# Attention units on an even timetable, and the last channel weights rounded at their use

## The chip, the core and the metric

The kernel runs on one core of a Trainium2 chip. A core has five engines with a queue each: PE multiplies matrices (its weight loads are listed apart as PEld), DVE, ACT and POOL work element by element, and SP issues the DMAs here. Each of DVE, ACT, POOL and SP takes its instructions in the order written; an instruction that waits holds up all behind it on its engine. The metric is device time in microseconds of one launch, the median of three runs.

## The reference

Three stages work on a batch of 4 sequences of 768 steps. The first is a gated linear attention with 8 heads of 48 channels, the second a block that mixes along the sequence, the third a mixer of tokens and then of channels.

```python
for t in range(S):                                   # attention, per batch and head
    state = f[t][:, None] * state + outer(k[t], v[t])
    y[t] = q[t] @ state
x = y.transpose(0, 2, 1, 3).reshape(B, S, H * D)     # 384 channels
h = np.maximum(x @ w_in, 0)                          # second stage
u, v = h[..., :512], h[..., 512:]
v_n = (v - mean(v)) / sqrt(var(v) + 1e-6)
v_s = einsum('ts,bsd->btd', w_spatial, v_n) + b_spatial[None, :, None]
x = (u * v_s) @ w_out
xt = x.transpose(0, 2, 1)                            # third stage
u = x + (np.maximum(xt @ w_tok1, 0) @ w_tok2).transpose(0, 2, 1)
out = u + np.maximum(u @ w_ch1, 0) @ w_ch2
```

The weights of the input block, of the output of the second stage, and of the third stage come as 64-bit floats; `f`, `k`, `q`, `v` and `w_spatial` come as 32-bit ones.

## The kernel before

Every product is made of three fp32r matmuls: each operand is split in a rounded part (names ending in `h`) and what is left of it (`l`), and `mm3` (L191, matmuls at L195 to L197) adds h·h, h·l and l·h in PSUM.

**Attention units.** The recurrence is cut into units, one for each batch, half of the sequence (`hf`) and pair of heads (`p`, 0 to 3): 32 units, numbered 0 to 31, eight to a batch. A unit is a Python generator, `att_unit` (L390), with five parts between its yields. Part 1 loads the unit's inputs (`fkq`, L400; with p = 0 also `vt`, L259), takes sigmoids on ACT and two scans on DVE (L269, L274), and scales keys and queries (L277). Part 2 is on PE: transposed keys `pt` (L283) and the products of keys and queries `pa` (L292), which ACT copies and POOL masks (`am`, L296, L297). I call it the unit's keys. Part 3 is PE's products of keys and values `pk` (L306, L307) and on DVE the chain of states `z` and `state` (L316 to L330). Part 4 is PE's product of queries and states, `py` (L338). Part 5 adds masked products times values into the same `py` (L346); I call it the sums. Then ACT and DVE split `py` into two parts (L422, L423). `py` has a single PSUM buffer, so the product with states of one unit waits until DVE has read the sums of the unit before.

**Gap rows.** The units with p = 0, 1, 2 write their 96 rows of `py` straight into the tiles `xh` and `xl` of their half. The rows that 64 - 48 leaves open are filled from the fourth unit: its parts `yh` and `yl` go through 12 DMAs of 16 rows each (L424 to L428), issued by SP. So the first use of a half's `xh` and `xl` waits for these.

**Tiles of the second stage.** For a half of a batch `s1` has three tiles `norm` (L480: nine matmuls of 512 columns into `pv`) and four tiles `gate` (L503: nine of 384 columns into `pu`). For a batch `s23` has eight tiles `mix` (L517: 18 matmuls, `ps`) and six `out1` (L538: 12 matmuls, `px`). That is 28 tiles to a batch. The three PSUM buffers of `ps_m` serve them all; `mix` is read out by DVE, the others by ACT first.

**Order.** PE's order in this part is the order written (`manual_schedule`, L566). `weave` (L183) spreads a list of attention steps over a list of tiles. `joined` (L450) makes two steps for each unit k:

```python
before = [k - 1] * (k > ks[0])
out += [each(*before, k, k + 1), each(k, *before)]
```

The first step runs the product with states of unit k - 1, the keys of unit k and part 1 of unit k + 1; the second runs part 3 of unit k and the sums of unit k - 1. The other engines' order is chosen by the scheduler.

**Weights of 64 bits.** `rounded` (L61) loads a piece of 128 rows (L64), puts its bits together on DVE (L69, L72), scales on ACT (L76) and adds on POOL (L77). Most third-stage weights are rounded early: `round_weight` (L89) makes pieces that store the result in DRAM (L100), and `more` (L461) runs one step of them behind each `gate` and `mix` tile from batch 1 on. Later `split_weight` (L134) loads the 32-bit copy (L153), rounds it to `h` on ACT (L155) and takes the rest `l` on POOL, or on DVE for `wc2` (L159). The staging tiles `wst` and `wsa` have three buffers each.

**Third stage.** `ff` (L699) runs twelve steps for each half: `up1` (`p`, then `hh` on ACT at L711 and `hl` on DVE at L712) and `down` (L724, `po`). POOL looks through all 64-bit weights for values near a threshold in the same steps (`look`, L123, three instructions for each of 88 pieces).

Of the kernel before, what the change touches and what calls it, by code (L numbers as in the profile page):

```python
# [18 lines left out]
def tile_kernel(ctx, tc, fkqs, v, w_in, w_sp, b_sp, w_out, w_t1, w_t2, w_c1, w_c2, out):  # L19
# [23 lines left out]
    def f32(ap):  # L43
        return ap.bitcast(F32)
# [154 lines left out]
    def body(general):  # L199
# [190 lines left out]
        def att_unit(b, hf, p):  # L390

            u = f"{b}{hf}{p}"
            t0 = hf * W
            fkq = at3.tile([P, 3 * W + 1 + NCW], F32, tag="fkq", name=f"fkq{u}")
            if (b, hf, p) == (0, 0, 0):
                for i in (2, 0, 1):
                    x = slice(i * W, (i + 1) * W + (i == 2) * (1 + NCW))
                    nc.sync.dma_start(out=fkq[:, x], in_=fkqs[b, p, hf, :, x])
            else:
                nc.sync.dma_start(out=fkq, in_=fkqs[b, p, hf])  # L400
            if p == 0:
                att_load_v(b, hf)
            fs = at2.tile([P, W + 1], F32, tag="fs", name=f"fs{u}")
            nc.scalar.activation(fs, fkq[:, 2 * W : 3 * W + 1], AF.Sigmoid)
            starts = fs[:, :W:C] if general else first[:, ::C]
            nc.scalar.activation(starts, fkq[:, 3 * W + 1 :], AF.Sigmoid)  # L406
            core = scanned if general else chunked
            py = yield from core(u, b, hf, p, fs, fkq, vts[b, hf])

            if p == 0:  # L410
                xt[b, hf] = (
                    xtp.tile([P, NK, W], F32R, tag="xh", name=f"xh{b}{hf}"),
                    xtp.tile([P, NK, W], F32R, tag="xl", name=f"xl{b}{hf}"),
                )
            xh, xl = xt[b, hf]
            if p < NK:
                yh, yl = xh[:, p, :], xl[:, p, :]
            else:
                yh = attp.tile([P, W], F32R, tag="yh", name=f"yh{u}")
                yl = attp.tile([P, W], F32R, tag="yl", name=f"yl{u}")  # L420
            pyf = py.rearrange("p c t -> p (c t)")
            nc.scalar.copy(yh[:112], pyf[:112])  # L422
            nc.vector.tensor_tensor(out=yl[:112], in0=pyf[:112], in1=f32(yh[:112]), op=ALU.subtract)  # L423
            if p == NK:  # L424
                for src, dst in ((yh, xh), (yl, xl)):
                    for m in range(2 * NK):
                        r0, w0 = 64 * (m // NK) + GAP * (m % NK), D + 64 * (m % 2)
                        nc.sync.dma_start(out=f32(dst[w0 : w0 + GAP, m // 2, :]), in_=f32(src[r0 : r0 + GAP, :]))  # L428

        units = [(b, hf, p) for b in range(B) for hf in range(2) for p in range(NP)]  # L430
        gens = {}
# [15 lines left out]
                out += [each(k + 1), each(k), each(k), each(k, k)]  # L447
            return out

        def joined(ks):  # L450

            out = []
            for k in ks:
                before = [k - 1] * (k > ks[0])
                out += [each(*before, k, k + 1), each(k, *before)]
            return out + [each(ks[-1], ks[-1])]

        st1 = {}
        early = []
# [11 lines left out]
        def s1(b, hf):  # L471
# [6 lines left out]
            d["u", hf] = us = up.tile([P, NJ, W], F32, tag="u", name=f"u{b}{hf}")  # L478

            def norm(i):  # L480
                xh, xl = xt[b, hf]
                ps = ps_m.tile([P, DH], F32, tag="m", name=f"pv{b}{hf}{i}")
                tsl = slice(i * P, (i + 1) * P)
                mm3(ps, [(xh[:, c, tsl], xl[:, c, tsl], winh[:, c, DH:], winl[:, c, DH:]) for c in range(NK)])
# [16 lines left out]
                nc.vector.tensor_tensor(out=d["vl"][:, s, :], in0=vf, in1=f32(d["vh"][:, s, :]), op=ALU.subtract)  # L501

            def gate(j):  # L503
                xh, xl = xt[b, hf]
# [62 lines left out]
        done = 2 * NP  # L567
        second, sa = joined(range(NP, done)), staged(st_a)
        weave(second[:4], sa[:6])
        weave(s1(0, 0), second[4:], sa[6:])  # L570
        out_steps = staged(st_b)
        rest = []
        for name, src in (("wt1", w_t1), ("wt2", w_t2), ("wc1", w_c1), ("wc2", w_c2)):
            kept[name], x = round_weight(wst, src, f"{name}{int(general)}", general)
            early += x
        early[:] = staged(list(early))
        for b in range(B - 1):
            a, (m, last_out) = s1(b, 1), s23(b)
            ks = range(done, done + NP + 1)
            steps = joined(ks)  # L580
            cut = len(steps) * len(a) // len(a + m)
            weave(a, steps[:cut], out_steps if b == 0 else [])
            weave(m, steps[cut:])
            x = s1(b + 1, 0)
            for i, y in enumerate(last_out):
                x.insert(2 + 3 * i, y)
            done = 2 * NP * (b + 2)
            weave(x, joined(range(ks[-1] + 1, done)))
        while early:
            early.pop(0)()  # L590
        right.close()
# [174 lines left out]
        h3p = e(tc.tile_pool(name="h3p", bufs=4))  # L766
        op = e(tc.tile_pool(name="op", bufs=2))
        otp = e(tc.tile_pool(name="otp", bufs=3))
        c2h, c2l, st_c = split_weight(w3p, wst, kept["wc2"], "wc2", NF, DM, nc.vector)
        st_c = staged(by_block[2 * NK : 3 * NK] + st_c[:3] + by_block[3 * NK :] + st_c[3:])  # L770
        weave(c2(0), st_c[:12])
        for b in range(B):
# [65 lines left out]
```

## Time and profile before

| | us |
|---|---|
| median of three runs (840.52 to 844.2) | 844.14 |
| the profiled execution | 838.88 |
| its span, first to last instruction | 837.1 |
| PE busy in the span | 772.7 |
| DVE, ACT, POOL busy | 392.1, 271.6, 365.6 |

The profile page lists the engines' busy time, and the trace can be asked for stretches of the span, for the order in time of one engine, and for what ended each idle time. Busy time of a stretch is no measure of its limit: what counts is which wait ended last. The granted clock of PE is the mean share of full speed in a stretch, between the two levels 1.2 and 2.4 GHz. Up to 47 us the first four units and the input weights are worked on; 47 to 93 us holds the first half of batch 0; then three stretches of eight units and 28 tiles follow, up to 411.9 us; the rest has no attention units.

### The profile page before, as it was taken

How to read it: one execution, taken by the hardware profiler on the slowest of the kernel's cores; microseconds unless marked ns; L12 is line 12 of the kernel's file. 1: busy time of each engine (PE TensorE's matmuls, PEld its weight loads, DVE VectorE, ACT ScalarE, POOL GpSimd, SP SyncE). 2: the span in 40 equal slices, each digit the busy share in tenths (PEclk: the TensorE clock that was granted, in tenths of full speed). 3: DMA queues.
4: the chain of work that ended last, by engine and by line, in shares of the span. 5: the costliest groups of instructions: out<-in, count | busy, mean ns of one | idle time of the engine just before them, and what ended most of it. 6: DMA issues, size and time to landing. Idle time of an engine off the chain costs nothing.

```text
span 837.1 us, 13044 instructions
## 1 busy us (share of the span) xinstructions
PE 772.7 (92%) x4860; PEld 713.9 (85%) x4860; DVE 392.1 (47%) x776; ACT 271.6 (32%) x602; POOL 365.6 (44%) x566
## 2 busy tenths in 40 slices
PE   5879799997979979889799999999999999999996
PEld 3557599885978858778699999999999999999996
DVE  6858467575785757876146251222122212222221
ACT  5556342343434424334353351112111311121110
POOL 3524220131542415424285279365935494547420
PEclk9889899998989979999899999999999999999999
DMA  7653321333646454543253162213221322113111
GB/s 254 192 173 120 100 70 33 125 106 107 190 127 200 137 161 135 178 125 98 81 162 94 58 197 67 85 48 123 85 86 38 115 75 85 48 29 114 38 57 34
DMA packets 53289, 91.06 MB, mean 109 GB/s; under 512 B 6624, under 2 KB 43104, under 8 KB 53216
## 3 DMA queue, kind: packets, MB, share of 16 engines
q1 hardware_dynamic: 53216, 90.14, 34.8%
q8 instruction: 40, 0.66, 0.3%
q14 instruction: 33, 0.27, 0.1%
HBM read 72.02 MB, written 15.73 MB: 105 GB/s over the span
## 4 chain that ended last, share of the span: by engine, by line
PE 71%; DMA 12%; DVE 10%; issue 3%; ACT 1%; POOL 1%; SPq 1%; DVEq 0%; ACTq 0%; POOLq 0%
PE po L724 17%; PE p L197 7%; PE p L195 7%; PE p L196 7%; DMA fkq<-in_fkq 5%; PE ps L195 3%; PE ps L197 2%; PE pa L292 2%; PE ps L196 2%; DMA vt<-in_v 2%; PE py L338 2%; PE pv L197 2%; PE py L346 2%; PE pv L195 2%; PE pv L196 1%
## 5 line engine op out<-in xcount | busy, mean ns | idle before, releaser
L712 DVE SCALAR_TENSOR_TENSOR hl<-p,hh 128x384 fp32r<-128x384 f32 x96 | 53.4, 557 | 187.2 <-ACT hh L711 181.9
L711 ACT ACTIVATE hh<-p 128x384 fp32r<-128x384 f32 x96 | 47.0, 490 | 196.8 <-PE p L197 196.8
L724 PE MATMUL po<-hl,wc2h 128*128 128x384 f32 x288 | 97.3, 338 | 0.4 <-DVE hl L712 0.4
L724 PE MATMUL po<-hh,wc2l 128*128 128x384 f32 x288 | 96.7, 336 | 0.0
L724 PE MATMUL po<-hh,wc2h 128*128 128x384 f32 x288 | 75.1, 337 | 0.1
L195 PE MATMUL ps<-wsph,vh 128*128 128x384 f32 x192 | 68.0, 354 | 0.0
L131 POOL TENSOR_SCALAR look<-look 128x192 f32<-128x192 f32 x88 | 62.8, 714 | 7.6
L197 PE MATMUL ps<-wsph,vl 128*128 128x384 f32 x192 | 65.9, 343 | 0.0
L196 PE MATMUL ps<-wspl,vh 128*128 128x384 f32 x192 | 65.9, 343 | 0.0
L197 PE MATMUL p<-uh,wc1l 128*128 128x384 f32 x192 | 65.0, 338 | 0.0
L130 POOL TENSOR_TENSOR look<-look 128x192 f32<-128x192 f32 x88 | 44.8, 511 | 45.9 <-DMA look<-in_w_c 25.6
L196 PE MATMUL p<-ul,wc1h 128*128 128x384 f32 x192 | 64.7, 337 | 0.0
L195 PE MATMUL p<-uh,wc1h 128*128 128x384 f32 x192 | 64.3, 338 | 0.0
L132 POOL TENSOR_TENSOR lows<-lows,look 128x192 f32<-128x192 f32 x88 | 53.1, 604 | 6.4
L735 POOL TENSOR_TENSOR us<-uh,ul 128x384 f32<-128x384 f32 x24 | 24.1, 1015 | 72.2 <-DVE ul L695 62.7
L297 POOL TENSOR_SCALAR_AFFINE_SELECT am<-am 128x384 f32<-128x384 f32 x64 | 38.7, 620 | 37.9 <-ACT am L296 37.6
L269 DVE TENSOR_TENSOR_SCAN pg<-fs,first 128x384 f32<-128x384 f32 x32 | 31.7, 992 | 50.2 <-ACT first L406 50.2
L724 PEld LDWEIGHTS po<-hl,wc2h 128*128 128x128 f32 x288 | 54.1, 188 | 0.7 <-DVE hl L712 0.7
L724 PEld LDWEIGHTS po<-hh,wc2l 128*128 128x128 f32 x288 | 54.1, 188 | 0.0
L724 PEld LDWEIGHTS po<-hh,wc2h 128*128 128x128 f32 x288 | 52.2, 188 | 0.4 <-ACT hh L711 0.4
L338 PE MATMUL py<-fkq,state 112*112 112x128 f32 x160 | 27.9, 298 | 21.8 <-DVE xl L423 10.8
L338 PEld LDWEIGHTS py<-fkq,state 112*112 112x112 f32 x160 | 23.1, 188 | 28.9 <-DVE xl L423 13.0
(332 smaller groups left out, 1976.9 us busy)
## 6 DMA issues: line engine op xcount, KB each, us to landing
fkq<-in_fkq SPq DMA_DIRECT2D x31, 578.0 KB, 4.1
look<-in_w_c SPq DMA_DIRECT2D x48, 192.0 KB, 2.3
vt<-in_v SPq DMA_DIRECT2D x8, 576.0 KB, 5.9
x1d<-xs SPq DMA_DIRECT2D x24, 192.0 KB, 2.0
xf<-x1d SPq DMA_DIRECT2D x12, 384.0 KB, 4.6
out<-ot SPq DMA_DIRECT2D x24, 192.0 KB, 2.0
look<-in_w_in SPq DMA_DIRECT2D x16, 192.0 KB, 3.2
look<-in_w_t SPq DMA_DIRECT2D x16, 192.0 KB, 2.4
```

The costliest lines, as they stand in the source:

```text
L130: nc.gpsimd.tensor_tensor(out=hi, in0=hi, in1=hi, op=ALU.mult)
L131: nc.gpsimd.tensor_scalar(out=hi, in0=hi, scalar1=NEAR**2, scalar2=None, op0=ALU.is_lt)
L132: nc.gpsimd.tensor_tensor(out=to, in0=to, in1=hi, op=ALU.add)
L195: nc.tensor.matmul(ps, lh, rh, start=first and i == 0, stop=False, **kw)
L196: nc.tensor.matmul(ps, lh, rl, start=False, stop=False, **kw)
L197: nc.tensor.matmul(ps, ll, rh, start=False, stop=i == n - 1, **kw)
L269: nc.vector.tensor_tensor_scan(out=pc, data0=fs[:, :W], data1=first, initial=0.0, op0=ALU.mult, op1=ALU.add)
L297: nc.gpsimd.affine_select(out=am[j], in_=am[j], compare_op=ALU.is_ge, fill=0.0, base=0, pattern=[[0, NCW], [1, C]], channel_multiplier=-1,)
L338: nc.tensor.matmul(py[:112, c, :], now[c][:112, :112], qi[:112, c * C : (c + 1) * C], start=c == n1, stop=False, skip_group_check=True,)
L711: nc.scalar.activation(hh, ps, AF.Relu)
L712: nc.vector.scalar_tensor_tensor(out=hl, in0=ps, scalar=0.0, in1=f32(hh), op0=ALU.max, op1=ALU.subtract)
L724: nc.tensor.matmul(po[c], l[:, ft, csl], r, start=ft == 0 and x == 0, stop=ft == NF - 1 and x == 2)
```

## The change

There are four parts.

1. The attention steps are no longer spread list by list. A timetable `turns` gives each step a tile number; `run` starts what is due before each tile. A batch has 28 tiles (`period`) and eight units, so a unit's first step comes every 3.5 tiles and its second half a unit later. All times are moved forward so that a half's last unit ends some tiles before that half's first `norm`, where before it ended one tile ahead.
2. The product with states (part 4) moves from the first step of a unit (`keys`) into the second (`sums`), right before part 3 of the next unit and its own sums. At the first unit of a batch (`i == 0`) it stays in `keys`, and the sums come there too.
3. `xh` and `xl` become one tile `x` with both parts side by side, and `yh`, `yl` one tile `y`. Six DMAs of 16 rows and both parts take the place of the twelve.
4. `wc2`, 12 pieces, is no longer rounded early and stored. `split_weight` rounds it where it is used, while `c2(0)` and `ff(0, 0)` run.

```diff
-                for src, dst in ((yh, xh), (yl, xl)):
-                    for m in range(2 * NK):
-                        r0, w0 = 64 * (m // NK) + GAP * (m % NK), D + 64 * (m % 2)
-                        nc.sync.dma_start(out=f32(dst[w0 : w0 + GAP, m // 2, :]), in_=f32(src[r0 : r0 + GAP, :]))
+                for m in range(2 * NK):
+                    r0, w0 = 64 * (m // NK) + GAP * (m % NK), D + 64 * (m % 2)
+                    nc.sync.dma_start(out=f32(x[w0 : w0 + GAP, m // 2]), in_=f32(y[r0 : r0 + GAP]))
...
+        def keys(k, before=False):
+
+            return each(*[k - 1] * before, k, *[k - 1] * before, k + 1)
+
+        def sums(k, before=True):
+
+            return each(*[k - 1] * before, k, *[k - 1] * before)
...
+        turns = [(-7, keys(k + 2)), (-6, sums(k + 2)), (-5, keys(k + 3)), (-4, sums(k + 3))]
+        period = 4 * NJ + 4 * NCW
+        for b in range(1, B):
+            for i in range(2 * NP):
+                k = 2 * NP * b + i
+                at = (b - 1) * period + i * period / (2 * NP) - (0 if general else 5)
+                then = at + period / (4 * NP)
+                if k < 2 * NP + 2 and not general:
+                    at, then = 2 * i - 3, 2 * i - 2
+                turns += [(at, keys(k, i == 0)), (then, sums(k, i > 0))]
+        turns += [((B - 1) * period - (0 if general else 5), each(k, k))]
...
+            for m in main:
+                while turns and turns[0][0] <= now[0]:
+                    turns.pop(0)[1]()
+                m()
+                now[0] += 1
...
-        for name, src in (("wt1", w_t1), ("wt2", w_t2), ("wc1", w_c1), ("wc2", w_c2)):
+        for name, src in (("wt1", w_t1), ("wt2", w_t2), ("wc1", w_c1)):
...
-        c2h, c2l, st_c = split_weight(w3p, wst, kept["wc2"], "wc2", NF, DM, nc.vector)
+        c2h, c2l, st_c = split_weight(w3p, wst, w_c2, "wc2", NF, DM, nc.vector, tiny=general)
```

The first place is on PE, in the tiles of batch 0's first half. `state` marks the product with states, `pt` and `pa` the keys, `pk` part 3 and `am` the sums. Before, unit 6's product with states is followed by unit 7's keys, and after a `gate` tile by unit 7's `pk` and unit 6's sums:

```order
L338 MATMUL py_821<-fkq_599,state_129 112x128
L338 MATMUL py_821<-fkq_599,state_130 112x128
L338 MATMUL py_821<-fkq_599,state_127 112x128
L283 MATMUL pt_825<-ident,fkq_703 128x112 x2
L292 MATMUL pa_830<-fkq_703 128x128
...
L195 MATMUL pu_869<-xh_231,winh 128x384
...
L306 MATMUL pk_880<-vt_431,kn_828 64x48
...
L346 MATMUL py_821<-am_691,vt_431 64x128
```

In the changed kernel the same unit's product with states stands behind unit 7's keys and a whole `norm` tile, directly ahead of unit 7's `pk` and its own sums:

```order
L283 MATMUL pt_756<-ident,fkq_659 128x112 x2
L292 MATMUL pa_761<-fkq_659 128x128
...
L195 MATMUL pv_802<-winh,x_231 128x512
...
L338 MATMUL py_826<-fkq_587,state_129 112x128
L338 MATMUL py_826<-fkq_587,state_130 112x128
L338 MATMUL py_826<-fkq_587,state_127 112x128
L306 MATMUL pk_830<-vt_430,kn_759 64x48
...
L346 MATMUL py_826<-am_647,vt_430 64x128
```

Between the sums of one unit and the product with states of the next there is now a full unit's distance; before it was half of one.

The second place is on PE, at the end of batch 0's first half: the sums of unit 7 (`am`), which the gap rows come from, and the first `norm` (`pv`) of the second half. Before, one piece of weights and one `gate` tile stand between them:

```order
L346 MATMUL py_915<-am_833,vt_431 48x128
L163 MATMUL wsppl_942<-wspsa_862,ident 128x384
L164 MATMUL wsppl_942<-wsph,minus 128x384
L195 MATMUL pu_946<-xh_231,winh 128x384
...
L197 MATMUL pu_946<-xh_231,winl 128x384
L195 MATMUL pv_965<-winh,xh_642 128x512
```

In the changed kernel three `gate` tiles (`pu`), four pieces of weights, and work of the units 8 and 9 stand between them:

```order
L346 MATMUL py_868<-am_764,vt_430 48x128
L163 MATMUL wsppl_919<-wspsa_793,ident 128x384
...
L195 MATMUL pu_930<-x_231,winh 128x384
...
L306 MATMUL pk_941<-vt_777,kn_876 64x48
...
L195 MATMUL pu_960<-x_231,winh 128x384
...
L283 MATMUL pt_971<-ident,fkq_907 128x112 x3
...
L195 MATMUL pu_1007<-x_231,winh 128x384
...
L338 MATMUL py_1022<-fkq_775,state_127 112x128
...
L306 MATMUL pk_1025<-vt_777,kn_975 64x48
...
L346 MATMUL py_1022<-am_881,vt_777 48x128
L195 MATMUL pv_1052<-winh,x_634 128x512
```

At the ends of batch 0's second half and of the later halves the distance is of the same kind.

The third place is on DVE, where `ff(0, 0)` begins. Before, the queue holds the `hl` of each step and one instruction (L159) for each piece of `wc2`:

```order
L712 SCALAR_TENSOR_TENSOR hl_5156<-p_5145,hh_5155 128x384
L712 SCALAR_TENSOR_TENSOR hl_5191<-p_5180,hh_5190 128x384
L159 TENSOR_TENSOR wc2l<-wc2sa_5178,wc2h 128x384
...
L159 TENSOR_TENSOR wc2l<-wc2sa_5210,wc2h 128x384
L159 TENSOR_TENSOR wc2l<-wc2sa_5280,wc2h 128x384
L712 SCALAR_TENSOR_TENSOR hl_5225<-p_5214,hh_5224 128x384
```

In the changed kernel the two rounding instructions of each piece (L69, L72) stand among them, and the first of these waits for its piece's DMA:

```order
L732 SCALAR_TENSOR_TENSOR hl_5045<-p_5034,hh_5044 128x384
L715 TENSOR_TENSOR ul_4829<-p_4954,uh_4828 128x384
L69 TENSOR_SCALAR wc2sa_5031<-wc270st 128x384
L72 SCALAR_TENSOR_TENSOR wc2sa_4991<-wc260st,wc2sa_4991 128x384
L159 TENSOR_TENSOR wc2l<-wc2sa_4951,wc2h 128x384
L72 SCALAR_TENSOR_TENSOR wc2sa_5031<-wc270st,wc2sa_5031 128x384
L69 TENSOR_SCALAR wc2sa_5068<-wc280st 128x384
L732 SCALAR_TENSOR_TENSOR hl_5084<-p_5073,hh_5083 128x384
```

Nine of the twelve pieces stand this way among `c2(0)` and `ff(0, 0)`; the first three stand earlier, among the `mix` tiles of batch 3.

## Rows read from the trace of the kernel before

**Rows 1.** The page's part 1: busy us, share, and instructions.

```profile
PE 772.7 (92%) x4860; PEld 713.9 (85%) x4860; DVE 392.1 (47%) x776; ACT 271.6 (32%) x602; POOL 365.6 (44%) x566
```

**Rows 2.** Waits of PE up to 500 us: total us, times, longest.

```profile
PE pv L195 <- DMA xh<-yh: 15.3, 4, 5.5
PE py L338 <- DVE xl L423: 10.8, 7, 3.6
...
PE py L338 <- DVE state L316: 5.9, 4, 3.2
PE py L338 <- DVE yl L423: 4.9, 4, 2.1
PE pv L197 <- DMA xl<-yl: 3.9, 4, 3.0
...
PE wsppl L163 <- DMA wspsa<-in_w_sp: 2.3, 1, 2.3
```

**Rows 3.** Stretches: length, then busy of PE, PEld, DVE, ACT, POOL; PEclk, DMA, GB/s.

```profile
120.19:150.26 30.07, 30.07 (x231) 28.17 (x230) 17.25 (x38) 8.67 (x22) 3.36 (x8) 1.00 0.22 67
93.41:196.18 102.77, 94.91 (x686) 83.25 (x687) 62.44 (x139) 37.88 (x90) 21.19 (x44) 0.96 0.29 89
196.18:306.38 110.20, 98.07 (x674) 85.81 (x675) 77.02 (x159) 43.05 (x98) 41.19 (x67) 0.92 0.50 153
306.38:411.90 105.52, 95.30 (x675) 83.47 (x675) 69.60 (x146) 41.50 (x91) 39.56 (x65) 0.95 0.40 127
```

**Rows 4.** Stretches at the start of the third stage, with the same columns.

```profile
480.00:500.00 20.00, 19.50 (x113) 18.75 (x113) 11.32 (x19) 10.99 (x23) 14.15 (x16) 1.00 0.68 208
500.00:530.00 30.00, 30.00 (x173) 30.00 (x172) 6.77 (x13) 4.42 (x9) 21.78 (x36) 1.00 0.31 86
```

**Rows 5.** PE in order of time, 84 to 110 us: start, us, instruction, idle before.

```profile
85.20 0.87 PE L346 MATMUL py<-am,vt 128*64 128x128 f32 x12
...
93.41 0.76 PE L195 MATMUL pv<-winh,xh 128*128 128x512 f32 x1 [4.76 <-DMA xh<-yh]
...
96.28 0.63 PE L197 MATMUL pv<-winh,xl 128*128 128x512 f32 x1
96.70 0.63 PE L195 MATMUL pv<-winh,xh 128*128 128x512 f32 x1
...
100.25 0.40 PE L195 MATMUL pv<-winh,xh 128*128 128x512 f32 x1
100.48 0.40 PE L196 MATMUL pv<-winl,xh 128*128 128x512 f32 x1
...
107.76 0.34 PE L196 MATMUL pu<-xl,winh 128*128 128x384 f32 x1
107.93 0.34 PE L197 MATMUL pu<-xh,winl 128*128 128x384 f32 x1
```

**Rows 6.** SP's DMA issues at the end of batch 0's first half.

```profile
87.31 3.68 SPq L428 DMA_DIRECT2D xh<-yh  x6
91.15 4.81 SPq L428 DMA_DIRECT2D xl<-yl  x6
```

**Rows 7.** DVE at 55 us, the remainder of a unit's sums.

```profile
55.77 0.56 DVE L423 TENSOR_TENSOR xl<-py,xh 112x384 fp32r<-112x384 f32 x1
```

**Rows 8.** Longest rounding instructions of a weight piece on DVE, 95 to 420 us.

```profile
L72 DVE SCALAR_TENSOR_TENSOR wc10da<-wc10d01152st,wc10da 128x384 uint32<-128x384 uint32 x1 | 1.4, 1384 | 0.0
...
L69 DVE TENSOR_SCALAR wc20da<-wc20d30st 128x384 uint32<-128x384 uint32 x1 | 1.2, 1171 | 0.5 <-POOL am L297 0.5
```

**Rows 9.** The same on POOL, 196 to 306 us.

```profile
L77 POOL TENSOR_TENSOR wt20da<-wt20da,wt20d00st 128x384 uint32<-128x384 uint32 x1 | 1.9, 1887 | 1.1 <-ACT wt20d00st L76 1.1
```

**Rows 10.** Instructions on wc2h: ns shortest, median, longest.

```profile
L155 ACT CAST wc2h<-wc2sa x12: 502/513/517, 474.5 to 496.6; 128x384 fp32r<-128x384 f32 x12
L159 DVE TENSOR_TENSOR wc2l<-wc2sa,wc2h x12: 540/558/1391, 475.1 to 497.1; 128x384 fp32r<-128x384 f32 x12
```

**Rows 11.** The chain that ended last: a load of a 64-bit piece on it.

```profile
348.33 5.09 DMA wc20d60st<-in_w_c
```

More of the change, by code (lines that the diff above doesn't have):

```diff
@@ L410, in att_unit @@
             if p == 0:
[L411 to L420, printed above, removed]
+                xt[b, hf] = xtp.tile([P, NK, 2, W], F32R, tag="x", name=f"x{b}{hf}")
+            x = xt[b, hf]
+            y = x[:, p] if p < NK else attp.tile([P, 2, W], F32R, tag="y", name=f"y{u}")
+            yh, yl = y[:, 0, :], y[:, 1, :]
             pyf = py.rearrange("p c t -> p (c t)")
@@ L448, in apart @@
             return out
[L450 to L456, printed above, removed]
+        def keys(k, before=False):
+            return each(*[k - 1] * before, k, *[k - 1] * before, k + 1)
+        def sums(k, before=True):
+            return each(*[k - 1] * before, k, *[k - 1] * before)
         st1 = {}
@@ L480, in norm @@
             def norm(i):
-                xh, xl = xt[b, hf]
+                xh, xl = (xt[b, hf][:, :, k, :] for k in range(2))
                 ps = ps_m.tile([P, DH], F32, tag="m", name=f"pv{b}{hf}{i}")
@@ L503, in gate @@
             def gate(j):
-                xh, xl = xt[b, hf]
+                xh, xl = (xt[b, hf][:, :, k, :] for k in range(2))
                 ps = ps_m.tile([P, W], F32, tag="m", name=f"pu{b}{hf}{j}")
@@ L566, in body, with run, also @@
         ordered.enter_context(tc.manual_schedule(engines={mybir.EngineType.PE}))
[L567 to L570, printed above, removed]
+        k = NP
+        sa = staged(st_a)
+        weave([keys(k), sums(k, False), keys(k + 1), sums(k + 1)], sa[:6])
+        turns = [(-7, keys(k + 2)), (-6, sums(k + 2)), (-5, keys(k + 3)), (-4, sums(k + 3))]
[9 more added lines that the diff above has]
+        turns += [((B - 1) * period - (0 if general else 5), each(k, k))]
+        now = [-7]
+        def run(main):
+            for m in main:
[3 more added lines that the diff above has]
+                now[0] += 1
+        def also(main, filler):
+            return [
+                lambda n=n, m=m: [
+                    x() for x in filler[len(filler) * n // len(main) : len(filler) * (n + 1) // len(main)] + [m]
+                ]
+                for n, m in enumerate(main)
+            ]
+        run(also(s1(0, 0), sa[6:]))
         out_steps = staged(st_b)
-        rest = []
-        for name, src in (("wt1", w_t1), ("wt2", w_t2), ("wc1", w_c1), ("wc2", w_c2)):
+        for name, src in (("wt1", w_t1), ("wt2", w_t2), ("wc1", w_c1)):
             kept[name], x = round_weight(wst, src, f"{name}{int(general)}", general)
@@ L578, in body @@
             a, (m, last_out) = s1(b, 1), s23(b)
[L579 to L583, printed above, removed]
+            run(also(a, out_steps if b == 0 else []))
+            run(m)
             x = s1(b + 1, 0)
@@ L586, in body @@
                 x.insert(2 + 3 * i, y)
-            done = 2 * NP * (b + 2)
-            weave(x, joined(range(ks[-1] + 1, done)))
+            run(x)
+        while turns:
+            turns.pop(0)[1]()
         while early:
```

## The prediction

> **What bounds the kernel now.** I began with the page's busy times: PE is busy for 772.7 of 837.1 us [rows 1], far ahead of the others, so the kernel is a stream of matmuls, and what can be won is PE's 64 us of idleness and whatever makes its matmuls slow. Next came the waits of PE [rows 2]. Two kinds stand out. The first `norm` of a half waits for the gap rows, on four occasions each for `xh` and `xl`: 15.3 + 3.9 = 19.2 us. The product with states (L338) waits for DVE, for the `xl` or `yl` that frees `py` and for `state`: 10.8 + 4.9 + 5.9 = 21.6 us. All of it lies in the first 500 us; behind that PE is full [rows 4].
>
> The third reading is how fast the matmuls go. Behind the wait of 4.76 us at 93.41, matmuls of 512 columns start 0.42 us apart; from about 100 us on it is 0.23 [rows 5]. That is the lower of the two clock levels, then the upper. The stretches show it as well: 1.00 where PE was never idle, but 0.96, 0.92 and 0.95 over the three stretches of eight units, whose waits fall in between [rows 3]. So a long wait costs twice: its own length, and slow matmuls behind it.
>
> **The change part by part.** *Gap rows.* Before, one `gate` tile (9 x 0.17 = 1.6 us [rows 5]) and at batch 0 one weight piece stand between the fourth unit's sums and `norm`. SP alone needs 3.68 us for six issues and 4.81 for the other six [rows 6]. After, six issues carry both parts, so some 4.8 us at most, plus the split ahead of them and the landing behind. The order gives three `gate` tiles, units' work and weight pieces as distance at batch 0 (4.7 us of `gate` alone, and about 10 with the rest), and two `out1` tiles (12 matmuls of 0.17, 2.1 us each) beside three `gate` tiles and units' work at the others, 9 to 10 us. The sums ended at 85.20 + 0.87 = 86.07 [rows 5], the first issue came 1.2 us later [rows 6], and `norm` began 7.3 us behind the sums with the first six landed. With both parts in six issues some 8 us are needed, the second part being 0.56 later on DVE [rows 7]; that fits with 1 to 2 us to spare. What would be late next is SP's queue: the `fkq` and `vt` loads stand ahead of the six issues, as before. I take all 19.2 us; the bounds are 10 (half of the waits return) and 19.2.
>
> *Product with states.* Its two needs, `py` read out and `state` computed, were met half a unit ahead; now a unit, 11 us at 28 tiles a batch. The longest wait seen was 3.6 us [rows 2], so the added half unit covers it. I take all 21.6, with 10 as the lower bound. Where a batch begins, however, the product follows the previous sums after one tile (1.6 us of `gate`). The read-out alone takes some 0.5 us on ACT and 0.56 on DVE [rows 7], and DVE has `z` and `state` in between. I put 1 us on each of four such places, 4 in all; bounds 0 and 4 x 3.6 = 14.
>
> *The wait for `w_spatial`* (2.3 us [rows 2]) came from twelve gap issues ahead of a load on SP; the load now stands ahead of six. I take 2.3. In exchange unit 5's keys now stand ahead of unit 4's product, at a place where DVE may not be ready: between 0 and the longest wait for DVE, 3.6 [rows 2]; I take 2.
>
> *Slow matmuls.* From the clock column the lost share is 0.04 x 102.8 + 0.08 x 110.2 + 0.05 x 105.5 = 18.2 us [rows 3]; part of that lies in the waits themselves. From the work it is more. The clean stretch of 30.07 us holds five `mix`, three `out1` and three units; at 0.174 a matmul the tiles make 126 x 0.174 = 21.9, which leaves 2.7 a unit; I use 2.9, for units of the second half have a third state. A batch then needs 288 x 0.174 + 54 x 0.23 + 8 x 2.9 = 85.7 us of PE. PE was busy 94.9, 98.1 and 95.3, together 288.3, against 257 and about 4 for four pieces of `w_out`: 27 us more. The bounds are thus 3 (if every idle us was slow) and 27; I take 18, nearer to the second. A clock that stays at 1.00 for 30 us with PE full says that it needs no rest.
>
> *DVE as the next limit.* In batch 1's stretch DVE is busy for 77 of 110.2 us [rows 3], and it has the same work there after. If PE needs 86, DVE stands at 90%, in order, with rounding pieces whose first instruction waits for a load of up to 5.1 us [rows 11]. PE's distances of 11 us take most of this. I put 5 us on it, bounds 0 and 12 (the idleness of that stretch now). In batch 2 the pieces of `wc2` leave DVE.
>
> *`wc2` at its use.* Twelve stores and reads of 32-bit copies go; twelve times L69, L72, L76, L77 come to the start of the third stage. DVE is busy there for 11.3 of 20 us and 6.8 of 30 [rows 4]. Nine pieces bring 9 x 2 x 0.56 = 10 us by the median of an instruction of that size [rows 10], at most 9 x (1.38 + 1.17) = 23 [rows 8]. Three staging buffers hold a piece from load to POOL's add: 5.1 + 1.2 + 1.4 + 1.9 = 9.6 at the longest [rows 8, 9, 11], 3.2 per piece, against a step of `ff` of 18 matmuls, 3.1. So it about keeps up at the worst, and the pieces start six tiles early. PE's small wait for `hl` there, 0.4, may become some us: taken at 2, bounds -0.4 and 8.
>
> Here the Trainium skill speaks against the change. The rows show that an L159 of 0.56 us at the median took up to 1.39 [rows 10], and POOL is busy for 21.8 of 30 us [rows 4]. The page "SBUF — State Buffer", section "Who interferes with whom", says that a DVE instruction with two inputs in SBUF and a POOL instruction that reads SBUF exclude each other, the later one waiting for the whole of the other. L72 has two such inputs, and is moved to where POOL is busiest. By that rule the nine pieces cost DVE 23 us rather than 10; the trace agrees with it in the longest rows, but the median doesn't show it.
>
> *Leftovers.* 2 us for the clock behind new waits.
>
> The sum: 19.2 + 21.6 + 2.3 + 18 = 61.1 us gained; 4 + 2 + 5 + 2 + 2 = 15 given back; net 46.1. The profiled execution took 838.88, so 792.8. That execution lies 5.3 under the median of the runs and 1.6 under the lowest; halfway, 3.4 on top makes 796.2, say 796.
>
> **The rivals.** *DVE's queue takes the waits over.* The distances help only if DVE works off its queue in time; if its in-order loads hold it in batches 0 to 2, half of the 21.6 and a third of the 18 are won, and the new costs come at 10 and not 5: 19.2 + 10.8 + 2.3 + 6 - 20 = 18.3, which gives 820.6 and with the 3.4 on top 824. For it speaks 77 of 110 busy; against it that PE was never idle from 120 to 150, and that the units are now as far apart as they can be. Chance 0.12.
>
> *The `ff` start is crowded.* DVE spends 23 us rather than 10 on the pieces, `hl` comes late for five or six steps, and PE waits 8 us and is slow behind it for 4: 12 in place of 2, so 806. For it: the longest rows and POOL's load; against: the margin, since the last piece is needed eleven steps of 3.1 us behind the first. Chance 0.12.
>
> *Slower.* The pieces of `wc2` go through one after the other: if the three buffers are held by pieces that wait for each other's turn on DVE, POOL and SP, each takes load, rounding, add, copy and remainder, 5.1 + 1.2 + 1.4 + 1.9 + 0.5 + 1.4 = 11.5 us, against a step of 3.1: nine pieces then cost 9 x 8.4 = 75 us. With the 46.1 + 2 won, that is 27 slower than the profiled execution, 870 with the 3.4. It decides from 3.1 + 48 / 9 = 8.4 us a piece. Against it speaks that three buffers exist and the queues interleave. Chance 0.03.
>
> *The change doesn't do what it says.* The order shows the distances, so only a wait that these don't touch can undo it, say SP's queue being late with `fkq`, so that keys wait where sums did: all of 21.6 and 18 would be given back, and 838.9 - 21.5 + 15 = 832.4, 836 with the 3.4. Chance 0.05.
>
> **How the numbers follow.** The forecast has 0.68. All kind bounds at once would gain 70 us and give back nothing, 772; they won't meet, and I set its lower end at 779. Its upper end is 812, with the lower bound of the gap rows or of the product with states, or DVE's 12. The crowded start lies inside these. The range is 779 to 825, which takes in the DVE rival; outside are the slower one, the undone change and the forecast's tails, under 0.2. About 0.5% can be told from no change here, 4.2 us: faster means under 839.9. The forecast, both middle rivals and half of the last are faster, 0.94; within 0.5% is 0.03, the rest of the last; slower is 0.03.
>
> **What the profile will show.** The first `norm` of the four halves starts without a wait for the gap DMA, and six issues take 3.7 to 4.8 us. L338's waits fall from 21.6 to some 4, and what is left sits one tile behind a batch's beginning. PEclk is 0.98 or more in the three stretches, and these take 90 to 95 us each. The last unit's sums end well ahead of 411 us, at some 360. Between there and the end PE is full but for a few us at the start of `ff(0, 0)`. It would be wrong if L338 or the keys wait for DVE in batch 1, if `norm` waits for SP, or if `hl` waits behind L69.

## The result, and the profile after

The changed kernel takes 799.65 us (median of four runs, 797.51 to 802.19) against 843.32 us (median of four; the 844.14 of the table is that of the first three); the ratio is 0.9489, with an interval of 0.9445 to 0.9532. The forecast was 796, in a range of 779 to 825. The profiled execution took 802.19 us, with a span of 800.5, so it is one of the longer runs; on another chip, beside the experiments, the same kernel took 797.73 (797.55 to 798.87).

Part 1 of the page, as in [rows 1]: PE is busy 16 us less for the same 4860 matmuls, since fewer of them run at the lower clock, and idle for 44 us in place of 64.

```profile
PE 756.9 (95%) x4860; PEld 709.4 (89%) x4860; DVE 406.6 (51%) x776; ACT 269.9 (34%) x602; POOL 370.8 (46%) x556
```

The waits of PE behind 40 us (total, times, longest), which answer to [rows 2]; these are the first three of eleven. In the rows, L417 is what L423 was, L744 what L724 was, and L732 what L712 was:

```profile
PE py L338 <- DVE x L417: 9.3, 4, 6.9
PE pt L283 <- issue: 3.0, 1, 3.0
PE po L744 <- DVE hl L732: 2.3, 2, 1.5
```

The waits for gap rows and for `w_spatial` are gone, and none for `state` is left. The eight that are not shown, 7.9 us together and none above 1.9, are waits for DVE or ACT at other instructions; the kernel before has none of them. Of the four waits for DVE's remainder one makes up most: 6.9 us.

The three stretches between the first `norm` tiles of the second halves, as in [rows 3] (length, busy PE, PEld, DVE, ACT, POOL, PEclk, DMA share, GB/s), then two short ones around that wait:

```profile
90.24:183.05 92.81, 90.11 (x659) 81.36 (x659) 64.54 (x136) 38.63 (x92) 27.02 (x45) 1.00 0.31 95
183.05:288.93 105.88, 95.30 (x675) 85.72 (x675) 79.17 (x160) 42.27 (x98) 41.78 (x68) 0.92 0.51 158
288.93:373.75 84.82, 84.82 (x634) 78.25 (x634) 55.21 (x117) 35.34 (x80) 23.95 (x42) 1.00 0.31 92
...
260.00:270.96 10.96, 3.94 (x38) 3.19 (x36) 9.35 (x22) 5.33 (x14) 5.38 (x9) 0.79 0.38 130
271.00:280.00 9.00, 9.00 (x45) 8.17 (x46) 7.93 (x12) 3.48 (x8) 3.33 (x6) 0.50 0.45 130
```

They took 102.77, 110.20 and 105.52 us before. The third is what all three could be: PE without a gap for 84.8 us, at the upper clock. The first comes close. The second is barely shorter than before, and it holds nearly all that is left to win in the three. There PE stands for 6.9 us, and for 9 us behind that every matmul runs at a granted clock of 0.50, the lower of the two levels (1.2 GHz). PE in order of time (start, us, instruction, idle before) shows both (a matmul of 384 columns takes 0.52 us at 279.17 and 0.34 at 280.23), and three of the four first `norm` tiles, which start with no idle time ahead:

```profile
48.96 0.61 PE L283 MATMUL pt<-ident,fkq 112*128 112x112 f32 x2 [2.97 <-issue]
...
90.24 0.50 PE L195 MATMUL pv<-winh,x 128*128 128x512 f32 x1
...
169.18 0.91 PE L338 MATMUL py<-fkq,state 112*112 112x128 f32 x6 [0.99 <-DVE x L417]
...
183.05 0.39 PE L195 MATMUL pv<-winh,x 128*128 128x512 f32 x1
...
261.38 0.88 PE L346 MATMUL py<-am,vt 128*48 128x128 f32 x12
...
270.96 1.62 PE L338 MATMUL py<-fkq,state 112*112 112x128 f32 x6 [6.91 <-DVE x L417]
...
279.17 0.52 PE L195 MATMUL px<-wouth,gh 128*128 128x384 f32 x1
...
280.23 0.34 PE L196 MATMUL pu<-x,winh 128*128 128x384 f32 x1
...
288.93 0.39 PE L195 MATMUL pv<-winh,x 128*128 128x512 f32 x1
```

Why 6.9 us? The sums of unit 22 end at 262.26 and the product with states of unit 23 stands one tile behind them. It needs `py` to be read out, by L417 on DVE. DVE's own order around it:

```profile
260.92 0.36 DVE L69 TENSOR_SCALAR wc10da<-wc10d1768st 128x384 uint32<-128x384 uint32 x1 [1.66 <-issue]
...
262.14 0.53 DVE L72 SCALAR_TENSOR_TENSOR wc10da<-wc10d1768st,wc10da 128x384 uint32<-128x384 uint32 x1
...
265.06 0.78 DVE L72 SCALAR_TENSOR_TENSOR wc10da<-wc10d11152st,wc10da 128x384 uint32<-128x384 uint32 x1
265.76 0.95 DVE L277 TENSOR_TENSOR fkq<-fkq,pg 128x768 f32<-128x768 f32 x1
...
270.35 0.55 DVE L417 TENSOR_TENSOR x<-py,x 112x384 fp32r<-112x384 f32 x1
```

DVE is hardly idle from 261 to 270, but L417 is the last of all that stands there: two rounding pieces, a unit's scans and the statistics of three `norm` tiles go first. At the beginning of the batch before, where no rounding piece is in the queue, the same wait is 0.99 us.

### The profile page after: what moved, and what is told of

It is laid out like the page before. It is cut to its first block, busy times and chain, and to the rows that moved or that the text cites. A ratio compares the mean times of both kernels' runs of the same rounds, so it can differ in the third digit from the quotient of the medians.

```text
span 800.5 us, 12918 instructions
## 1 busy us (share of the span) xinstructions
PE 756.9 (95%) x4860; PEld 709.4 (89%) x4860; DVE 406.6 (51%) x776; ACT 269.9 (34%) x602; POOL 370.8 (46%) x556
## 4 chain that ended last, share of the span: by engine, by line
PE 72%; DVE 8%; DMA 8%; POOL 4%; issue 4%; ACT 3%; SPq 1%; DVEq 0%; POOLq 0%; ACTq 0%
PE po L744 18%; PE p L197 8%; PE p L196 8%; PE p L195 8%; DMA fkq<-in_fkq 4%; PE ps L195 3%; PE ps L197 3%; PE ps L196 3%; PE pa L292 2%; PE py L338 2%; PE py L346 2%; PE px L195 2%; PE px L196 2%; PE px L197 2%; PE pu L195 1%
## 5 line engine op out<-in xcount | busy, mean ns | idle before, releaser
L732 DVE SCALAR_TENSOR_TENSOR hl<-p,hh 128x384 fp32r<-128x384 f32 x96 | 53.2, 556 | 176.0 <-ACT hh L731 165.1
L744 PE MATMUL po<-hl,wc2h 128*128 128x384 f32 x288 | 97.5, 338 | 2.3 <-DVE hl L732 2.3
L744 PE MATMUL po<-hh,wc2l 128*128 128x384 f32 x288 | 96.7, 336 | 0.0
L744 PE MATMUL po<-hh,wc2h 128*128 128x384 f32 x288 | 75.0, 336 | 0.0
L297 POOL TENSOR_SCALAR_AFFINE_SELECT am<-am 128x384 f32<-128x384 f32 x64 | 44.2, 707 | 38.0 <-ACT am L296 37.7
L272 POOL COPY pend<-pg 128x3 f32<-128x3 f32 x32 | 10.7, 335 | 107.7 <-DVE pg L269 100.5
L744 PEld LDWEIGHTS po<-hl,wc2h 128*128 128x128 f32 x288 | 54.1, 188 | 3.3 <-DVE hl L732 3.3
L744 PEld LDWEIGHTS po<-hh,wc2l 128*128 128x128 f32 x288 | 54.1, 188 | 0.0
L744 PEld LDWEIGHTS po<-hh,wc2h 128*128 128x128 f32 x288 | 52.3, 188 | 0.0
L195 PEld LDWEIGHTS ps<-wsph,vh 128*128 128x128 f32 x192 | 36.6, 190 | 4.7 <-ACT vh L493 1.6
```

Of the source, the lines that this page charges most:

```text
L195: nc.tensor.matmul(ps, lh, rh, start=first and i == 0, stop=False, **kw)
L297: nc.gpsimd.affine_select(out=am[j], in_=am[j], compare_op=ALU.is_ge, fill=0.0, base=0, pattern=[[0, NCW], [1, C]], channel_multiplier=-1,)
L732: nc.vector.scalar_tensor_tensor(out=hl, in0=ps, scalar=0.0, in1=f32(hh), op0=ALU.max, op1=ALU.subtract)
L744: nc.tensor.matmul(po[c], l[:, ft, csl], r, start=ft == 0 and x == 0, stop=ft == NF - 1 and x == 2)
```

## Experiments

Each run has its own measure of the kernel before on its chip (839.0, 839.33 and 840.01 us in the three groups); I give the median, and the ratio to that measure. The changed kernel has 0.9489, and 0.9453 (0.9376 to 0.953) beside the last group. Where a run is compared with the changed kernel, the difference is one of medians from different chips, unless I say beside; told from the kernel before on each chip, the losses of the next runs come out 1 to 4 us larger.

**One part alone, or one part undone.** First the merged gap rows alone, in the kernel before:

```diff
-                for src, dst in ((yh, xh), (yl, xl)):
-                    for m in range(2 * NK):
...
+                for m in range(2 * NK):
...
+                    nc.sync.dma_start(out=f32(x[w0 : w0 + GAP, m // 2]), in_=f32(y[r0 : r0 + GAP]))
```

> The kernel before with one part of the change alone: both parts of a gap row side by side, six DMAs in place of twelve; units and tiles stand where they stood. If it is the distance between the last sums and the first norm that matters, the six issues still take 3.7 to 4.8 us, both parts now wait for the remainder on DVE (0.56 us), the waits for the first part stay at about 15 us and only the 3.9 us for the second part go, with little of the slow clock: 838 to 842 against 843. If the number of DMAs is what made the first norm late, most of the 19.2 us and half of the slow matmuls behind it go: about 815.

838.21 us, ratio 0.9975 (0.9948 to 1.0002): no difference to be told. The waits of PE:

```profile
PE pv L195 <- DMA x<-y: 21.0, 6, 7.0
```

Before they were 15.3 + 3.9 = 19.2 [rows 2]. Half as many DMAs don't bring the rows sooner to the first `norm`, which now needs both parts. Then the lead undone:

```diff
-                at = (b - 1) * period + i * period / (2 * NP) - (0 if general else 5)
+                at = (b - 1) * period + i * period / (2 * NP)
...
-                if k < 2 * NP + 2 and not general:
+                if False:
...
-        turns += [((B - 1) * period - (0 if general else 5), each(k, k))]
+        turns += [((B - 1) * period, each(k, k))]
```

> The changed kernel with the units' times moved back: none of the five tiles ahead, so that a half's last sums stand right ahead of the half's first norm; six DMAs, the moved state products and the late wc2 stay. If the lead is what hides the gap rows, the first norm of the three later halves waits some 7 to 8 us each, and matmuls behind each wait run at the lower clock: 25 to 35 us more than the changed kernel, 825 to 835. If the merged DMAs alone suffice, it stays within 5 us of the changed kernel, about 803.

824.6 us, ratio 0.9815, the first case: 25 us of the gain are gone. Of the waits for DVE few are left, and the gap rows are waited for in five places:

```profile
PE pv L195 <- DMA x<-y: 29.8, 5, 9.1
PE py L338 <- DVE x L417: 2.7, 2, 2.0
```

So it is the distance, not the number of DMAs. The product with states, put back to the keys:

```diff
         def keys(k, before=False):
-            return each(*[k - 1] * before, k, *[k - 1] * before, k + 1)
+            return each(k - 1, k, *[k - 1] * before, k + 1)
         def sums(k, before=True):
-            return each(*[k - 1] * before, k, *[k - 1] * before)
+            return each(k, *[k - 1] * before)
...
-        weave([keys(k), sums(k, False), keys(k + 1), sums(k + 1)], sa[:6])
+        weave([each(k, k + 1), sums(k, False), keys(k + 1), sums(k + 1)], sa[:6])
```

> The changed kernel with the product with states back in the step of the next unit's keys, half a unit behind the sums before it; the even timetable, the lead and the rest stay. If the distance of a whole unit is what took the waits for DVE away, L338 waits 10 to 20 us in all again and slow matmuls come back behind them: 812 to 825. If the even spacing alone did it, L338 waits no more than in the changed kernel (9.3 us, of them 6.9 in one place) and the time is the same within 4 us.

827.7 us, ratio 0.9871, above the range of the first case: 28 us of the gain are gone. L338 waits for 30.4 us in all, more than before the change and than the 10 to 20 that I expected, although units are evenly spaced:

```profile
PE py L338 <- DVE x L417: 21.1, 10, 4.2
PE py L338 <- DVE state L316: 8.3, 5, 4.7
...
PE py L338 <- DVE y L417: 1.0, 1, 1.0
```

Even spacing does not do it; the place behind a whole unit does. Then the pieces of `wc2`, rounded early again:

```diff
-        for name, src in (("wt1", w_t1), ("wt2", w_t2), ("wc1", w_c1)):
+        for name, src in (("wt1", w_t1), ("wt2", w_t2), ("wc1", w_c1), ("wc2", w_c2)):
...
-        c2h, c2l, st_c = split_weight(w3p, wst, w_c2, "wc2", NF, DM, nc.vector, tiny=general)
+        c2h, c2l, st_c = split_weight(w3p, wst, kept["wc2"], "wc2", NF, DM, nc.vector)
```

> The changed kernel with its last part undone: the 12 pieces of wc2 rounded early and stored, as before. By my sum the late rounding costs 2 us at its use (two waits for hl, 2.3 us in the trace of the changed kernel) and saves DVE work in the batches; the early pieces come after those of wc1, so mostly behind 289 us, where PE was never idle for 85 us: 797 to 803, no difference that can be told from the changed kernel's 800. If DVE has no room for them there, the third stretch (84.8 us, full) gets waits: 805 to 815. If the crowding at the use is worth more than the waits show, 790 to 795.

808.18 us, ratio 0.9635 (0.9613 to 0.9657): 8 to 10 us slower than the changed kernel, the second of the three cases. The third stretch, and what stands in it:

```profile
286.34:385.39 99.05, 90.38 (x634) 82.23 (x633) 68.79 (x141) 38.71 (x86) 39.76 (x61) 0.95 0.43 133
...
371.77 1.62 PE L338 MATMUL py<-fkq,state 112*112 112x128 f32 x6 [5.51 <-DVE x L417]
```

With the pieces in it, this stretch has the same wait at its end as the second one has, and takes 14.2 us more. Behind it, from 385.39 to the end, this version needs 420.21 us where the changed kernel needs 426.75. So rounding late costs 6.5 us behind the stretches and saves 14 in the third. Of the 6.5 only 1.5 are waits for `hl` (2.3 us against 0.8); 2.7 are waits for ACT and DVE between 383 and 393 us that this version does not have. The other way round, late rounding alone in the kernel before (the same two lines):

> The kernel before with the last part of the change alone: wc2 rounded where it is used. If it is a small matter, it loses 1 to 3 us at the start of the last stage and wins some of the waits of batch 2's second half, where the pieces stood: 835 to 842 against 839. If DVE's rounding is what makes the product with states wait there (9.8 us of L338's waits fall between 329 and 392 us), about half of these and slow matmuls behind them go: 825 to 832.

834.2 us, ratio 0.995 (0.993 to 0.9969): a gain of 5 us, a little more than the first case had. The third stretch falls from 105.52 to 94.38 us and the rest grows from 425.20 to 429.80, the same two sides again.

**The long wait.** I tried its two suspects apart. First the distance: no rule for a batch's first unit.

```diff
-                turns += [(at, keys(k, i == 0)), (then, sums(k, i > 0))]
+                turns += [(at, keys(k)), (then, sums(k))]
```

> The changed kernel without the rule for the first unit of a batch: there too the product with states and the sums of the unit before come half a unit after the keys, so that they stand a whole unit behind the sums before. If the one long wait left (6.9 us at 264 us, for DVE's remainder of the sums, and 10 us of matmuls at the lower clock behind it) comes from the short distance at this place, it goes, with some 5 us of slow matmuls: 10 to 12 us less, about 788 to 790, unless a norm now waits for the gap rows, which have 1.75 tiles less. If DVE is so full there that it would be late anyway, the wait moves behind the next tile and the time stays within 3 us of 800.

800.43 us, ratio 0.9525: no gain. L338 waits nowhere any more behind 40 us, and the second stretch is 5 us shorter, 100.68; but PE now waits at the same place for the next unit's keys, and the parts ahead of it and behind it lose what it wins (the first stretch begins 3.3 us later, the third takes 1.6 us more):

```profile
268.12 0.79 PE L283 MATMUL pt<-ident,fkq 112*128 112x112 f32 x3 [2.77 <-issue]
```

The keys need L277, which on DVE ends at 268.0: DVE is late with everything here. The first `norm` waits for gap rows again, too, 2.4 us in two places: their lead is shorter. So next DVE's load, with the early pieces begun in batch 0, and later only behind `mix` tiles:

```diff
-            if b and early:
+            if early:
...
-                more(b, us[:, j, :1])
+                if b == 0:
+                    more(b, us[:, j, :1])
```

> The changed kernel with the early rounding pieces spread: they begin at batch 0 (behind its second half's gate tiles and its mix tiles, 12 places that had none) and go on behind mix tiles only, so that some 8 of the 17 pieces in the second stretch (183 to 289 us) leave it. The timetable and the batch beginnings stay. If DVE's full queue causes the wait of 6.9 us at 264 us (it has no idle time of note from 261 to 274), this wait falls under 3 us, the second stretch takes 90 to 95 us in place of 105.9, and the time is 785 to 792; part may come back in the first stretch. If the short distance at a batch's beginning is the cause by itself, the wait stays at 5 us or more and the time at 797 to 803.

802.94 us, ratio 0.9565: that theory fell. DVE's work in the second stretch is down from 79.2 to 70.2 us, yet the wait is there as before, and a second one has come where pieces now stand in the first stretch:

```profile
176.99 1.62 PE L338 MATMUL py<-fkq,state 112*112 112x128 f32 x6 [6.82 <-DVE x L417]
...
276.61 1.62 PE L338 MATMUL py<-fkq,state 112*112 112x128 f32 x6 [6.82 <-DVE x L417]
```

So it is not how much DVE has to do in the stretch as a whole; what stands in its queue at a batch's beginning was the next suspect. With both edits:

> The pieces spread as in the run before, and the even batch beginnings of the earlier run (no rule for a batch's first unit). If DVE's load is the cause and the distance no more than where it shows, this is within 3 us of the run with the spread pieces alone. If both count, it is 4 to 6 us faster than that one, about 783 to 787. If the first norm now waits for the gap rows, as in the earlier run (2.4 us in two places), it may be 2 to 4 us slower.

795.1 us, ratio 0.9459: 8 us better than the spread alone, so both count, though the time is not the 783 to 787 that I expected. The two long waits for L417 become waits of 2.7 and 2.8 us for the keys. Then the queue by itself: the changed kernel without rounding steps behind the last two `mix` tiles of a batch.

```diff
-                more(b, g[:, :1])
+                if hf == 0 or j < 2:
+                    more(b, g[:, :1])
```

> The changed kernel, but no step of the early rounding behind the last two mix tiles of a batch, so that no rounding pieces stand in DVE's queue where the next batch begins; the pieces come later, the number is the same, and the rule for a batch's first unit stays. In the changed kernel the product with states at a batch's beginning waited 0.99 us where no piece stood ahead of the remainder of the sums (169 us), and 6.91 where two did (264 us). If short distance and pieces in the queue make the long wait together, it falls to 1 to 3 us here, the matmuls behind it run at the upper clock, and the second stretch is some 8 to 10 us shorter: 789 to 793. If two units and three norms fill the queue there without the pieces, the wait stays at 5 us or more and the time at 798 to 803.

795.54 us against 797.73 of the changed kernel beside it. The wait falls only to 4.24, between the two cases, though no piece stands ahead of L417. One row of PE and one of DVE:

```profile
264.90 1.47 PE L338 MATMUL py<-fkq,state 112*112 112x128 f32 x6 [4.24 <-DVE x L417]
...
256.83 0.96 DVE L277 TENSOR_TENSOR fkq<-fkq,pg 128x768 f32<-128x768 f32 x1
```

What is the rest? PE's order is the same as at 169 us of the changed kernel, where the wait is 0.99. There DVE had waited for ACT for 1.84 us, had caught up, and its L277 began 1.4 us ahead of the batch's third `norm` (161.10 and 162.51). DVE of the changed kernel there:

```profile
158.45 0.96 DVE L269 TENSOR_TENSOR_SCAN pg<-fs,first 128x384 f32<-128x384 f32 x1 [1.84 <-ACT first L406]
...
161.10 0.96 DVE L277 TENSOR_TENSOR fkq<-fkq,pg 128x768 f32<-128x768 f32 x1
```

Here it begins 1.8 us behind that `norm` (256.83 and 254.99). DVE thus comes 3.3 us later to the batch's beginning, and 4.24 - 0.99 = 3.25 us is what the wait is longer. By these differences the 6.91 us would be made of 0.99 for the short distance with DVE in step, 3.25 because DVE comes behind, and 2.67 for the pieces in the queue. That is an estimate, since the rows are from two kernels and two places. What puts DVE behind by then I didn't take apart; pieces run in the tiles ahead of it, and in the quiet place at 169 us none do. The trace does show what DVE stood still for on the way, the loads of two pieces:

```profile
237.95 0.36 DVE L69 TENSOR_SCALAR wc10da<-wc10d10st 128x384 uint32<-128x384 uint32 x1 [2.48 <-DMA wc10d10st<-in_w_c]
...
242.76 0.36 DVE L69 TENSOR_SCALAR wc10da<-wc10d1384st 128x384 uint32<-128x384 uint32 x1 [2.93 <-DMA wc10d1384st<-in_w_c]
```

From the second of them to L277 at 256.83 it is idle for only 0.9 us more, so it does not catch up. No run took these loads away, so their share of the 3.25 us is not shown. The last two runs have the quiet beginning and the pieces spread from batch 0 on, now behind the second halves' `gate` tiles too, the second of them with the even beginnings as well:

```diff
-                more(b, us[:, j, :1])
+                if hf == 1 or b == 3:
+                    more(b, us[:, j, :1])
```

> The same quiet batch beginnings, and the pieces spread from batch 0 on (behind the gate tiles of second halves and the first six mix tiles), the rule for a batch's first unit as in the changed kernel. Where the spread alone had two waits of 6.82 us, both should now be 1 to 3 us: 786 to 793. If the queue is full without the pieces, 800 to 805 as with the spread alone.

803.5 us, ratio 0.9529, a miss again: two waits, of 4.23 and 4.25 us. With pieces in batch 0's tiles DVE is behind at the first beginning too; ahead of it L69 had waited for loads for 1.56 us at 144.33 and for 2.22 at 148.44.

> The run before with the even batch beginnings too (the product with states and the sums half a unit later at a batch's first unit). If the queue was the whole cause, it adds nothing or little: within 3 us of the run before. The waits of 2.7 us that the even version had for the keys at a batch's beginning should fall under 1 us, since DVE's scaled keys also stood behind the pieces: 784 to 792.

793.98 us (792.64 to 795.08), ratio 0.9404 (0.9327 to 0.9482). My forecast of at most 3 us less than the run before was wrong, and the time lies 2 us above its range: the even beginning brought 9.5 us. L338 and the keys wait nowhere in the stretches; the gap rows are waited for again, 3.1 us in four places, the longest 1.8 at 91.71:

```profile
91.71:185.14 93.43, 90.84 (x659) 81.16 (x659) 72.76 (x155) 39.42 (x97) 36.77 (x57) 1.00 0.44 134
185.14:280.19 95.05, 91.19 (x675) 81.91 (x675) 75.40 (x150) 38.85 (x93) 39.79 (x57) 0.98 0.47 144
280.19:365.60 85.41, 85.11 (x633) 78.18 (x634) 54.24 (x112) 34.04 (x78) 24.23 (x41) 1.00 0.28 83
```

The second stretch has come down from 105.88 to 95.05 us. A whole unit's distance at a batch's beginning takes the wait for L417, and with a queue without pieces there the keys are ready as well, at the price of a shorter lead for the gap rows.

> The changed kernel itself, on the chip of these runs, as their measure: 797 to 803, with the one long wait of 6 to 7 us at 264 us.

797.73 us; the long wait is 6.83 us here. All four runs of the last version lie under all four of the changed kernel, by 3.7 us in the medians. It has the lowest median of these kernels, though its runs overlap with those of the quiet beginning alone (793.94 to 797.54) and of the run with both edits (790.53 to 795.63).

## Why the prediction held, and where it did not

**Gap rows, 19.2 us.** Held in full: the first `norm` of no half waits. SP's six issues take 4.64, 3.68, 3.67 and 3.69 us, each with both parts. What wins here is the distance; the merging alone shows nothing.

```profile
80.97 4.64 SPq L421 DMA_DIRECT2D x<-y  x6
...
173.73 3.68 SPq L421 DMA_DIRECT2D x<-y  x6
...
277.71 3.67 SPq L421 DMA_DIRECT2D x<-y  x6
...
365.95 3.69 SPq L421 DMA_DIRECT2D x<-y  x6
```

**Product with states, 21.6 us, and 4 us given back at batch beginnings.** The first half held, and undoing the move shows it to be decisive. The second is the step that failed: L338's waits are 9.3 us, of which 8.5 stand at three of the four places (0.56 us at 75.64, 0.99 and 6.91; the fourth, at 363.18, has none). One is nearly twice the 3.6 us that I took as the longest possible, and it stands in batch 1's stretch, where I had called such a wait a sign of being wrong. I had put the read-out's own time there (0.5 on ACT and 0.56 on DVE) and named `z` and `state`, but not the scans, `norm` statistics and rounding pieces that stand ahead of it in DVE's order, nor that DVE may come to the place late.

**`w_spatial`, 2.3 us, and the early keys, 2 us.** Both right in size and place: unit 5's keys, the sixth in PE's order, wait 2.97 us at 48.96; DVE ends their scaling (L277) at 48.86 only.

**Slow matmuls, 18 us.** The three stretches need 318.5 us before and 283.5 after. Of the 35 us, 16.9 are idle time of PE (30.2 and 13.3) and 18.1 are busy time. But the stretches of after hold 67 recorded matmuls fewer, which the lead has moved ahead of them: 1.6 units of 41.6 matmuls, by my 2.9 us a unit an estimate of 4.7 us. That leaves about 13 us for the clock in the stretches, where the sum had 18 - 2 = 16. Over the whole kernel PE's busy time fell by 772.7 - 756.9 = 15.8 us, so the size was right and some of it lies outside the stretches. My need of a batch, 85.7, was near: the third stretch is 84.82 us with 41 matmuls of units fewer than the second, 2.9 us by the same estimate, so 87.7.

**DVE as the next limit, 5 us.** Right as a thing to fear, and too small: beside L338, the keys and `hl`, PE has 7.9 us of new waits, 3.7 for DVE and 4.2 for ACT. Each stretch was to take 90 to 95 us at a clock of 0.98 or more. The first does, the third is better, and the second takes 105.88 at 0.92: 10.6 us of idle time and, against 87.7, 7.6 of slow matmuls. The rival of the DVE queue came true at one place of the three stretches, not throughout.

**`wc2` at its use, 2 us.** PE's waits for `hl` are 2.3 us as forecast, but the stages behind the last stretch are 6.5 us longer than with early rounding (within the bounds, -0.4 to 8; against the kernel before they are 1.6 us longer, 425.20 and 426.75). On the other side the sum had no term at all for the pieces that leave DVE in the third stretch; in the changed kernel these are worth 14 us. I called the part a small loss, and it is a gain of 5 alone and of 8 to 10 in the changed kernel. The total didn't suffer, because I had already counted all waits there as won by the moved product; they could only go with both.

The rule against this part, of the Trainium skill, page "SBUF — State Buffer", section "Who interferes with whom", fared better than I gave it credit for. In the stretch where nine pieces come, DVE and POOL are both nearly full, and the rounding instructions are long:

```profile
440.00:472.00 32.00, 29.66 (x168) 28.36 (x168) 27.74 (x36) 14.98 (x31) 28.54 (x28) 1.00 0.51 157
...
443.73 1.26 DVE L72 SCALAR_TENSOR_TENSOR wc2sa<-wc230st,wc2sa 128x384 uint32<-128x384 uint32 x1
...
468.06 2.09 DVE L72 SCALAR_TENSOR_TENSOR wc2sa<-wc2110st,wc2sa 128x384 uint32<-128x384 uint32 x1
```

From the one row to the other there are nine L72, 11.8 us together, and with their L69 18.9: nearer to the 23 that I drew from the longest rows than to the 10 that I took. That agrees with two engines excluding each other, but no run here took POOL's work away, so it is not shown. L69 has only one input, and it too took up to 1.47 us here. Of the 18.9 us PE saw 2.3.

**The sum.** Net 46.1 us were forecast for the profiled execution, and 838.88 - 802.19 = 36.7 came. The clock's part came, 15.8 of 16, so what is missing is idle time of PE: it fell from 64.4 to 43.6 us, by 20.8, where the sum has 43.1 - 13 = 30.1. L338 makes 5.3 us of these 9.3, the new waits for DVE and ACT 2.9 (7.9, where I had 5), and the keys 1. Against the medians the gain is 43.7, since the profiled execution of after was a long one and that of before a short one. That the median, 799.65, came within 4 us of the 796 is thus in part luck: on the profiled executions, on which the sum was made, it was 9.4 off.

**The parts don't add up.** Undoing the lead costs 25 us, the moved product 28 and the late rounding 8 to 10; with the merge's 1 that is over 60, where all together gain 44. The parts overlap: the third stretch needs both the moved product and the late rounding, and a wait that comes back brings its slow matmuls too. How much each overlap is worth was not measured.

## What to carry to other kernels

When an instruction of a full engine waits for one of an in-order engine, count what stands ahead of that one in its queue, at that place, and not the time of that one alone; the price of a short distance is the queue. What that engine stood still for a few tiles earlier may belong to the count. Work that has no deadline (here the early rounding) is best kept out of the queue at the few places where a distance can't be long. And look at an even timetable's seams first: the one long wait that was left, and those of the runs above with the same beginnings, stood at the beginning of a batch.

## What was not expected of the chip

How hard a short wait hits: behind 0.99 us at 169 the clock stays at 1.00, behind 1.92 us at 232.01 the stretch from 232 to 238 us shows 0.72, behind 2.97 us at 48.96 the stretch from 48 to 54 us shows 0.50, and behind 6.91 us the lower clock lasts for 9 us although PE has no gap in them.

```profile
48.00:54.00 6.00, 5.04 (x20) 3.48 (x20) 4.14 (x6) 2.72 (x7) 1.55 (x3) 0.50 0.48 127
...
232.00:238.00 6.00, 5.99 (x41) 5.68 (x41) 5.79 (x9) 2.64 (x7) 3.01 (x5) 0.72 0.59 161
...
170.00:176.00 6.00, 6.00 (x55) 5.32 (x54) 3.96 (x7) 2.90 (x9) 2.30 (x3) 1.00 0.70 204
```

And a DMA issue costs SP the same with twice the data: six issues with one part took 3.68 and 4.81 us [rows 6], six with both parts 3.67 to 4.64.
